# Attention and a SwiGLU block on one core: scores computed transposed, exponentials without the row maximum, and feed-forward blocks of 384 and 512 tokens

## The chip, the cores and the metric

The kernel runs on one core of a Trainium2 chip. The metric is the device time of one execution in microseconds (us), taken as the median of several runs. The core has a matrix engine (PE, whose weight loads are listed apart as PEld), a vector engine (DVE), a scalar engine (ACT), a general engine (POOL) and a queue engine (SP) that here only issues transfers. Each engine works through its own instructions in order and waits on the others through semaphores.

## What is computed

```python
# q, k, v: 8 batches x 12 heads x 448 tokens x 64;  g_q, g_k: 64
q_n, k_n = rmsnorm(q, g_q), rmsnorm(k, g_k)
scores = q_n @ k_n^T / 8
scores = scores - max(scores, axis=-1)
attn = exp(scores);  attn = attn / (sum(attn) + 1e-9)
x = (attn @ v), heads side by side: 3584 tokens x 768
g = x @ w_gate                     # 768 x 1536
h = g * sigmoid(g) * (x @ w_val)   # 768 x 1536
out = h @ w_out                    # 1536 x 768
```

All of it is in float32. The three weight matrices come in as float64 and are rounded to float32 on the chip.

## The kernel before

A batch's 448 tokens lie on 112 partitions, four to each. Heads are taken in pairs, so that two heads of 64 fill 128 partitions of the transposed queries and keys. A step of the attention is half the queries (two chunks of 112) of a pair of heads; a batch has 12 steps, the whole kernel 96.

In a step `softmax` computes four tiles of scores (L208, queries on the partitions), takes the maximum of each row on DVE (L218), lets ACT form the exponentials with that maximum as bias and sum them (L222), and DVE divides them (L224 to L229). One step later `transpose_p` transposes the 16 blocks of the exponentials on PE (L240) and copies them out of PSUM on DVE and ACT (L242), and `weighted_sum` multiplies them with the values (L252, the two heads on the two halves of the partitions) and copies the result to `xT` (L259). Before every second step `normalise` scales the next pair of queries and keys (squares on POOL L166, sums on DVE L168, the power -1/2 on POOL L171, products on POOL L175) and `transpose_qk` transposes them (L190, copies L194 and L196).

The feed-forward block takes the tokens of one batch at a time. `gate_value` computes a tile of 128 hidden units for 448 tokens: six matmuls with `wg` and six with `wv` (L268), the silu on ACT (L273) and the product on DVE (L274). `out_rows` computes 112 tokens by 384 outputs from 12 matmuls (L283), copies them (L291) and stores them from SP (L294).

The order of the work is the order in which the program calls these functions: nothing reorders it. In step i the calls are `softmax(i)`, `normalise`, one unit of the feed-forward block of the batch before, `transpose_p(i - 1)`, the other units, `weighted_sum(i - 1)`, `transpose_qk`. The first batch's attention has no feed-forward work beside it. Instead it carries the weights: 36 parts of 768 KB are loaded by SP into four buffers, and three times a step `weights_step` issues the rounding of a part (DVE L126, L134, L147, L148; ACT L137, L138; POOL L151, L152). The feed-forward block of the last batch runs alone at the end.

Of the kernel before, what the change touches and what calls it, by code (L numbers as in the profile page):

```python
# [9 lines left out]
F32 = mybir.dt.float32  # L10
U32 = mybir.dt.uint32
I64 = mybir.dt.int64
AF = mybir.ActivationFunctionType
ALU = mybir.AluOpType
AX = mybir.AxisListType


@with_exitstack
def kernel(
    ctx: ExitStack,  # L20
    tc: tile.TileContext,
    q: bass.AP,
# [31 lines left out]
    NF = DFF // P  # L54
    HALF = DM // 2
    STEPS = 2 * NPAIR
    # The high word of 2**-126 as a float64, the least normal float32, read as a float32.
    TINY = 2.0**-15 * 1.125

    const = ctx.enter_context(tc.tile_pool(name="const", bufs=1))  # L60
# [33 lines left out]
        nc.sync.dma_start(vt[m].rearrange("p h j d -> p h (j d)"), pair_rows(v, m))  # L94

    def weight_parts():
        """Parts of the weights as they come in, and where they go."""
        gate, val = (w.rearrange("(c p) f -> p c f", p=P) for w in (moe_w_gate, moe_w_val))
        for c in range(NW):
            for half in range(2):  # L100
                for w, dst in ((gate, wg), (val, wv)):
                    yield w[:, c, ts(half, DFF // 2)], dst[:, c, ts(half, DFF // 2)]
        rows = moe_w_out.rearrange("(f p) c -> p f c", p=P)
        for f in range(NF):
            yield rows[:, f, :], wo[:, f, :]
# [5 lines left out]
            nc.sync.dma_start(raw, src)  # L111
            staged.append((raw.bitcast(U32).rearrange("p (n two) -> p n two", two=2), dst))

    # round_high and round_low make of a part's float64 bits the nearest float32. The float32 of
    # the high word's 20 bits of the fraction takes the high word's sign and first bit of the
    # exponent, and the bits behind the exponent's next three, which are all the first one's
    # opposite wherever the value is a normal float32; smaller values become 0. The low word times
    # its unit is added to that, and the sum is rounded.

    def round_high():  # L120
        if not staged:
# [35 lines left out]
        load_weights()  # L157

    def normalise(m):
        """Scales the pair's queries and keys by 1 / sqrt(sum of squares + 64 eps), that is by  # L160
        their inverse rms over 8; gg makes up for both eighths."""
        t = prep.tile([R, NJ, 2, 2, D], F32, name="qkn")
        sq = t.rearrange("p j x h d -> p (j x h d)").rearrange("p (g d) -> p g d", d=D)
        src = qk.pop(m)
        flat = src.rearrange("p x h j d -> p (x h j) d")
        nc.gpsimd.tensor_tensor(out=sq, in0=flat, in1=flat, op=ALU.mult)  # L166
        ss = prep.tile([R, 2 * 2 * NJ], F32, name="ss")
        nc.vector.tensor_reduce(out=ss, in_=sq, axis=AX.X, op=ALU.add)  # L168
        nc.vector.tensor_scalar_add(ss, ss, D * 1e-6)  # L169
        rr = prep.tile([R, 2, 2, NJ, 1], F32, name="rr")  # L170
        nc.gpsimd.tensor_tensor(  # L171
            out=rr.rearrange("p x h j one -> p (x h j one)"), in0=ss, in1=minus_half, op=ALU.pow
        )
        for x in range(2):
            nc.gpsimd.tensor_tensor(  # L175
                out=t[:, :, x].rearrange("p j h d -> p h j d"),
                in0=src[:, x],
                in1=rr[:, x].to_broadcast([R, 2, NJ, D]),
                op=ALU.mult,
            )  # L180
        qkn[m] = t
# [112 lines left out]
            nc.sync.dma_start(tokens[j], outsb.pop((b, j)))  # L294

    def ffn_plan(b):
        """The block's units by step: two hidden tiles a step in the first half, then the output's."""
        units = [[lambda f=f: gate_value(b, f) for f in (2 * n, 2 * n + 1)] for n in range(NF // 2)]
        outs = [lambda j=j, h=h: out_rows(b, j, h) for j in range(NJ) for h in range(2)]
        rest = STEPS - len(units)  # L300
        for n in range(rest):
            units.append(outs[n * len(outs) // rest : (n + 1) * len(outs) // rest])
        return units
# [54 lines left out]
            fn()  # L358


# [1 line left out]
_INS = ["q", "k", "v", "g_q", "g_k", "moe_w_gate", "moe_w_val", "moe_w_out"]  # L362
_OUTS = [((3584, 768), "float32")]
# [25 lines left out]
```

## Time and profile before

| | |
|---|---|
| median of 3 runs | 2389.96 us (2389.5 to 2390.48) |
| profiled execution, first to last instruction | 2387.6 us |
| PE busy | 2096.2 us, 88% |
| DVE busy | 945.6 us, 40% |
| ACT busy | 595.8 us, 25% |
| POOL busy | 479.3 us, 20% |
| first feed-forward matmul starts at | 342.4 us |
| transfers | 73.69 MB, 31 GB/s on average |

The profile lists groups of instructions by line and engine with their number, busy time and mean duration. It draws the span in 40 slices, with the share of the time an engine is busy in tenths and a row for the clock that PE was granted (9 is 90% and more of full speed). One float32 matmul of the program appears as two records on PE, a transpose as one. A timeline merges neighbouring records: the first number is the start, the second the length.

### The profile page before, as it was taken

What the parts mean: (1) busy time and instruction counts of PE and PEld (TensorE: products, weight loads), DVE (VectorE), ACT (ScalarE), POOL (GpSimd) and SP (SyncE); (2) the same over time, 40 slices, a digit from 0 to 9 for tenths busy, and PEclk for the clock granted to TensorE, in tenths of its full rate; (3) what the DMA queues carried; (4) which work ended last, traced back from release to release, by engine and by line L of the source; (5) the groups of instructions that cost most, each with busy time, mean ns of one, the idle gap of its engine ahead of it and who ended that gap; (6) DMA issues with size and microseconds to landing.
All of it is one profiled execution on the core that took longest, in us unless ns stands there. A gap on an engine that the chain in (4) does not pass through costs nothing.

```text
span 2387.6 us, 20461 instructions
## 1 busy us (share of the span) xinstructions
PE 2096.2 (88%) x8064; PEld 1111.7 (47%) x8064; DVE 945.6 (40%) x1713; ACT 595.8 (25%) x1246; POOL 479.3 (20%) x271
## 2 busy tenths in 40 slices
PE   3445469999999999999999999999999999999999
PEld 1222234455545554455445554455444554455555
DVE  6778853344233433344233433344233433332000
ACT  2333332322222222322222222322222222321000
POOL 5656641121111111121111111121111111110000
PEclk9655569999999999999999999999999999999999
DMA  3333300010000010000000010010000010000000
GB/s 123 107 102 93 126 27 12 12 29 24 18 23 12 24 35 12 12 30 24 18 24 12 24 35 12 12 30 24 18 24 12 24 35 12 12 22 12 6 0 24
DMA packets 44257, 73.69 MB, mean 31 GB/s; under 512 B 3712, under 2 KB 35968, under 8 KB 44160
## 3 DMA queue, kind: packets, MB, share of 16 engines
q1 hardware_dynamic: 43840, 72.37, 10.1%
q8 instruction: 64, 1.05, 0.2%
q14 instruction: 33, 0.27, 0.0%
q10 hardware_dynamic: 320, 0.00, 0.0%
HBM read 61.34 MB, written 11.01 MB: 30 GB/s over the span
## 4 chain that ended last, share of the span: by engine, by line
PE 76%; DVE 6%; ACT 3%; issue 1%; POOL 0%; DVEq 0%; ACTq 0%
PE mm L268 37%; PE mm L283 21%; PE sc L208 7%; PE av L252 6%; PE tr L240 4%; ACT p L222 3%; DVE nmax L218 2%; DVE pt L242 2%; PE tr L190 2%; DVE gt L274 1%; ACT pt L242 1%; DVE outsb L291 1%; POOL raw L151 0%; DVE wo L147 0%; DVE p L229 0%
## 5 line engine op out<-in xcount | busy, mean ns | idle before, releaser
L283 PE MATMUL mm<-wo,gt 128*112 128x384 f32 x1536 | 508.5, 488 | 0.0
L268 PE MATMUL mm<-xT,wg 128*128 128x448 f32 x1152 | 453.8, 543 | 0.0
L268 PE MATMUL mm<-xT,wv 128*128 128x448 f32 x1152 | 448.6, 539 | 0.0
L208 PE MATMUL sc<-KT,QT 64*112 64x448 f32 x768 | 282.8, 603 | 139.7 <-ACT p L222 138.9
L283 PEld LDWEIGHTS mm<-wo,gt 128*112 128x112 f32 x1536 | 267.2, 177 | 234.9 <-issue 28.0
L222 ACT ACTIVATE p<-sc,nmax 112x448 f32<-112x448 f32 x384 | 239.6, 630 | 495.7 <-DVE nmax L218 495.7
L171 POOL TENSOR_TENSOR rr<-ss,minus_half 112x16 f32<-112x16 f32 x48 | 142.7, 2972 | 1020.1 <-DVE ss L169 1020.1
L274 DVE TENSOR_TENSOR gt<-gt,mm 128x448 f32<-128x448 f32 x96 | 59.6, 621 | 676.0 <-PE mm L268 676.0
L268 PEld LDWEIGHTS mm<-xT,wv 128*128 128x128 f32 x1152 | 218.9, 190 | 214.1 <-issue 212.6
L240 PE MATMUL tr<-ident,p 112*112 112x112 f32 x1536 | 205.3, 279 | 121.0 <-DVE pt L242 113.1
L268 PEld LDWEIGHTS mm<-xT,wg 128*128 128x128 f32 x1152 | 212.1, 190 | 210.7 <-issue 210.5
L218 DVE TENSOR_REDUCE nmax<-sc 112x1 f32<-112x448 f32 x384 | 221.7, 618 | 127.3 <-PE sc L208 123.2
L240 PEld LDWEIGHTS tr<-ident,p 112*112 112x112 f32 x1536 | 166.6, 142 | 195.7 <-DVE pt L242 135.7
L242 ACT COPY pt<-tr 112x448 f32<-112x448 f32 x192 | 102.0, 531 | 508.4 <-PE tr L240 508.4
L208 PEld LDWEIGHTS sc<-KT,QT 64*112 64x112 f32 x768 | 90.3, 181 | 278.1 <-ACT p L222 210.8
L252 PE MATMUL av<-pt,v 112*64 112x224 f32 x1536 | 208.6, 387 | 4.3 <-ACT pt L242 4.3
L166 POOL TENSOR_TENSOR qkn<-qk 112x1024 f32<-112x1024 f32 x48 | 90.8, 1892 | 547.5 <-DMA qk<-in_k_dram 530.7
L242 DVE COPY pt<-tr 112x448 f32<-112x448 f32 x192 | 119.0, 620 | 125.8 <-PE tr L240 125.8
L252 PEld LDWEIGHTS av<-pt,v 112*64 112x64 f32 x1536 | 117.7, 147 | 96.3 <-issue 38.7
L229 DVE TENSOR_SCALAR p<-p,rsum 112x448 f32<-112x448 f32 x384 | 147.9, 449 | 3.4
L273 ACT ACTIVATE gt<-mm 128x448 f32<-128x448 f32 x96 | 52.1, 543 | 346.2 <-PE mm L268 346.2
L259 DVE COPY xT<-av 128x224 f32<-128x224 f32 x96 | 37.5, 391 | 239.1 <-PE av L252 239.1
(40 smaller groups left out, 988.2 us busy)
## 6 DMA issues: line engine op xcount, KB each, us to landing
qk<-in_q_dram SPq DMA_DIRECT2D x48, 224.0 KB, 3.7
qk<-in_k_dram SPq DMA_DIRECT2D x48, 224.0 KB, 3.7
v<-in_v_dram SPq DMA_DIRECT2D x48, 224.0 KB, 2.9
out_dram<-outsb SPq DMA_DIRECT2D x32, 336.0 KB, 2.7
raw<-in_moe_w_gate_dram SPq DMA_DIRECT2D x12, 768.0 KB, 4.6
raw<-in_moe_w_val_dram SPq DMA_DIRECT2D x12, 768.0 KB, 4.4
raw<-in_moe_w_out_dram SPq DMA_DIRECT2D x12, 768.0 KB, 4.4
gq<-in_g_q_dram ACTq DMA_DIRECT2D x2, 0.2 KB, 3.5
```

What stands on the lines that cost most here:

```text
L166: nc.gpsimd.tensor_tensor(out=sq, in0=flat, in1=flat, op=ALU.mult)
L171: nc.gpsimd.tensor_tensor(out=rr.rearrange("p x h j one -> p (x h j one)"), in0=ss, in1=minus_half, op=ALU.pow)
L208: nc.tensor.matmul(sc, QT[m][rows, 2 * half + jl, :], KT[m][rows].rearrange("p j r -> p (j r)"), start=True, stop=True,)
L218: nc.vector.tensor_reduce(out=nmax[:, at], in_=scs[hh], axis=AX.X, op=ALU.max, negate=True)
L222: nc.scalar.activation(p, scs[hh], AF.Exp, bias=nmax[:, at], accum_out=den[:, at])
L229: nc.vector.tensor_scalar(out=p, in0=p, scalar1=rsum[i][:, ds(2 * jl + hh, 1)], scalar2=None, op0=ALU.mult)
L240: nc.tensor.transpose(ps[0:R, j, :], p[:, ts(j, R)], ident[0:R, 0:R])
L242: copy(PT[i, hh][:, :, jl, :], ps[0:R])
L252: nc.tensor.matmul(av[ds(64 * hh, 64), :], vt[m][:, hh, j, :], PT[i, hh][:, j].rearrange("p a r -> p (a r)"), start=(j == 0), stop=(j == N ...
L268: nc.tensor.matmul(t, w[:, c, ts(f, P)], xT[b][:, c, :], start=(c == 0), stop=(c == NW - 1))
L274: nc.vector.tensor_tensor(out=g, in0=g, in1=ps[1], op=ALU.mult)
L283: nc.tensor.matmul(ps[0:R, 0:HALF], gt[b][:, f, ts(j, R)], wo[:, f, ts(half, HALF)], start=(f == 0), stop=(f == NF - 1),)
```

## The change

The old kernel stays in the program under the name `general`. A new function `fast` runs first. A guard takes the largest product of the two gains, and after `fast` all engines read a flag: if that product is above 8, `general` runs as well; otherwise its instructions are branched over. In the reference's inputs the largest product is 5.26.

`fast` computes the same result in another way:

- The scores are transposed: keys lie on the partitions, queries along the free dimension. The exponentials (one ACT instruction for two heads, 896 elements) are then already in the layout in which the weighted sum takes them, so the 1536 transposes of the exponentials and their copies are gone.
- No row maximum is subtracted. The maxima on DVE and the division of the exponentials are gone. The four tiles of exponentials of a pair are added up on POOL (three additions of 896 elements), a matmul with ones sums them over the partitions, and DVE takes the reciprocal and multiplies the weighted sum by it.
- A pair of heads is two slots. The even slot transposes the next pair's queries and keys, computes half the scores and the weighted sum of the pair before; the odd slot computes the other half and divides.
- The squares move from POOL to ACT, and the copy of the transposed keys from DVE to ACT.
- The feed-forward block takes two batches (896 tokens) as a block of 384 and one of 512 tokens. Output tiles have 128 tokens in place of 112: 56 tiles of 12 matmuls in place of 64. The silu is computed from a tanh on ACT, with one more DVE operation.
- The attention of the next two batches is spread over the first half of the 384 block (12 slots, one after every second unit) and the second half of the 512 block (12 slots over 16 half units). The other two halves and the last 512 block run with no attention beside them.
- The weights come in by groups of 256 hidden units, through the buffer `gt` in place of buffers of their own. A part is rounded by two instructions on ACT and four on DVE (none on POOL); the addition is an integer one on 16-bit halves. 20 of the 36 parts are rounded within the 14 slots that come before the first feed-forward unit, the rest between the first units.
- Outputs are stored from ACT's queue in place of SP's.

On PE in the steady part, before: the names are `mm` for the feed-forward tiles, `tr` for transposes, `av` for the weighted sum, `sc` for scores. The rows around the end of a step, from the first half of a feed-forward block:

```order
L268 MATMUL mm<-xT,wv 128x448 x6
L240 MATMUL tr<-ident,p 112x112 x16
L268 MATMUL mm<-xT,wg 128x448 x6
L268 MATMUL mm<-xT,wv 128x448 x6
L252 MATMUL av<-pt,v 64x224 x8
L190 MATMUL tr<-ident,qkn 128x112 x8
L208 MATMUL sc<-KT,QT 112x448 x4
L268 MATMUL mm<-xT,wg 128x448 x6
L268 MATMUL mm<-xT,wv 128x448 x6
L240 MATMUL tr<-ident,p 112x112 x16
```

The same place after the change, from the first half of a 384 block (L622 is the feed-forward matmul, L539 the transposes of queries and keys, L555 the scores, L575 the weighted sum, L588 the sum by ones):

```order
L555 MATMUL st<-QT,KT 112x448 x4
L588 MATMUL at<-sums,ones 64x448 x2
L622 MATMUL mm<-xT,wg 128x384 x6
L622 MATMUL mm<-xT,wv 128x384 x6
L539 MATMUL at<-ident,t 128x112 x8
L555 MATMUL st<-QT,KT 112x448 x4
L575 MATMUL at<-e,v 64x448 x8
L622 MATMUL mm<-xT,wg 128x384 x6
L622 MATMUL mm<-xT,wv 128x384 x6
```

The 32 transposes of the exponentials of a pair are gone, the two weighted sums of 224 columns have become one of 448, a sum by ones is new, and a slot stands after two feed-forward units instead of being split by them.

On DVE while the first batch's weights are rounded, before: L147 to L134 is the rounding of one part, L218 to L229 the softmax of a step.

```order
L147 SCALAR_TENSOR_TENSOR wg<-raw,wg 128x768
L148 TENSOR_SCALAR raw<-wg 128x768
L126 TENSOR_SCALAR wv<-raw 128x768
L134 SCALAR_TENSOR_TENSOR wv<-raw,wv 128x768
L218 TENSOR_REDUCE nmax<-sc 112x1 x4
L224 TENSOR_SCALAR den<-den 112x4
L225 RECIPROCAL rsum<-den 112x4
L229 TENSOR_SCALAR p<-p,rsum 112x448 x4
L168 TENSOR_REDUCE ss<-qkn 112x16
L169 TENSOR_SCALAR ss<-ss 112x16
```

After, in the slots before the first feed-forward unit (L482 to L494 is one part, L590 and L591 the division of a pair, L544 to L516 the next pairs' queries and sums of squares):

```order
L590 RECIPROCAL inv<-at 128x448
L591 TENSOR_TENSOR xT<-at,inv 128x448
L482 TENSOR_SCALAR wv<-wv 128x768
L483 TENSOR_SCALAR wv<-wv 128x768
L491 SCALAR_TENSOR_TENSOR wv<-gt,wv 128x768
L494 ISA wv<-gt,wv 128x1536
L544 TENSOR_SCALAR QT<-at,gg 128x448
L515 TENSOR_REDUCE ss<-t 112x16
L516 TENSOR_SCALAR ss<-ss 112x16
```

A pair of heads leaves five DVE instructions where it left 30, the addition of a weight part comes from POOL to DVE (L494), and the reciprocal of a whole tile is new.

The diff, cut to what the steps below speak of:

```diff
+def fast(ctx, tc, q, k, v, g_q, g_k, moe_w_gate, moe_w_val, moe_w_out, out):
+    BLOCKS = ((0, 384), (384, 512))
+    ps_st = ctx.enter_context(tc.tile_pool(name="ps_st", bufs=2, space=bass.MemoryType.PSUM))
+    ps_at = ctx.enter_context(tc.tile_pool(name="ps_at", bufs=2, space=bass.MemoryType.PSUM))
+    ps_mm = ctx.enter_context(tc.tile_pool(name="ps_mm", bufs=2, space=bass.MemoryType.PSUM))
...
+    def load_weights():
+        if not parts:
+            return
+        n = parts[0][0]
+        slot = n % 4 if n < 20 else 2 + n % 2
+        if any(slot == other[0] for other in staged):
+            return
...
+    def round_weights():
...
+        nc.scalar.activation(w, hi.bitcast(F32), AF.Abs)
+        nc.scalar.activation(lo, lo, AF.Copy, scale=2.0**-29)
+        nc.vector.tensor_scalar_max(w, w, LEAST)
+        nc.vector.tensor_scalar(out=bits, in0=bits, scalar1=3, scalar2=0x3FFFFFFF, ...)
+        nc.vector.scalar_tensor_tensor(bits, hi, 0xC0000000, bits, ...)
+        nc.vector.tensor_tensor(out=bits, in0=bits, in1=lo, op=ALU.add)
...
+    def scores(m, j):
+        st = ps_st.tile([P, 2, TB], F32, name="st")
+        for h in range(2):
+            rows = ds(D * h, D)
+            nc.tensor.matmul(st[0:R, h, 0:S], KT[m][rows, j, :], QT[m][rows]..., ...)
+        E[m, j] = attn.tile([R, 2, S], F32, name="e", bufs=5)
+        nc.scalar.activation(E[m, j], st[0:R, :, 0:S], AF.Exp)
+        if j == 1:
+            nc.gpsimd.tensor_tensor(out=sums[m], in0=E[m, 0], in1=E[m, 1], op=ALU.add)
+        elif j > 1:
+            nc.gpsimd.tensor_tensor(out=sums[m], in0=sums[m], in1=E[m, j], op=ALU.add)
...
+    def divide(m):
+        den = ps_at.tile([P, TB], F32, name="at")
+        for h in range(2):
+            nc.tensor.matmul(den[ds(D * h, D), 0:S], ones[0:R, :], s[:, h], ...)
+        nc.vector.reciprocal(inv, den[:, 0:S])
+        nc.vector.tensor_tensor(out=xT[...], in0=av.pop(m)[:, 0:S], in1=inv, op=ALU.mult)
+
+    def slot(i):
+        m, second = divmod(i, 2)
+        if not second:
+            transpose_qk(m + 1)
+        if m < NM:
+            for j in (0, 1):
+                scores(m, 2 * second + j)
+        if m > 0:
+            if second:
+                divide(m - 1)
+            else:
+                weighted(m - 1)
+                load_v(m + 1)
+        if not second:
+            normalise(m + 2)
+            load_qk(m + 3)
...
+    attend(PER + 2)                      # 14 slots; PER = 12
+    for n in range(B):
+        if n % 2 == 0:
+            mix(ups(n), PER)             # 24 units of 384 tokens, 12 slots between them
...
+            mix(downs(n), 0)
+        else:
+            mix(ups(n), 0)               # 24 units of 512 tokens
+            mix(downs(n), PER if n < B - 1 else 0)
...
+    fast(tc, *args)
+    fits = nc.values_load(fits[0:1, 0:1], min_val=0, max_val=1)
+    with tc.If(fits == 0):
+        general(tc, *args)
```

More of the change, by code (lines that the diff above doesn't have):

```diff
@@ L18, with general @@
 @with_exitstack
-def kernel(
+def general(
     ctx: ExitStack,
@@ new lines, with kernel @@
+@with_exitstack
+def kernel(
+    ctx: ExitStack,
+    tc: tile.TileContext,
+    q: bass.AP,
+    k: bass.AP,
+    v: bass.AP,
+    g_q: bass.AP,
+    g_k: bass.AP,
+    moe_w_gate: bass.AP,
+    moe_w_val: bass.AP,
+    moe_w_out: bass.AP,
+    out: bass.AP,
+):
+    nc = tc.nc
+    args = (q, k, v, g_q, g_k, moe_w_gate, moe_w_val, moe_w_out, out)
+    D = q.shape[3]
+    guard = ctx.enter_context(tc.tile_pool(name="guard", bufs=1))
+    g2 = guard.tile([1, 2, D], F32, name="g2")
+    gp = guard.tile([1, D], F32, name="gp")
+    top = guard.tile([1, 1], F32, name="top")
+    fits = guard.tile([1, 1], mybir.dt.int32, name="fits")
+    for i, x in enumerate((g_q, g_k)):
+        nc.scalar.dma_start(g2[:, i], x.rearrange("(one d) -> one d", one=1))
+    nc.vector.tensor_tensor(out=gp, in0=g2[:, 0], in1=g2[:, 1], op=ALU.mult)
+    nc.vector.tensor_reduce(
+        out=top, in_=gp, axis=AX.X, op=ALU.max, apply_absolute_value=True
+    )
+    nc.vector.tensor_scalar(out=fits, in0=top, scalar1=8.0, scalar2=None, op0=ALU.is_le)
+    fast(tc, *args)
+    fits = nc.values_load(fits[0:1, 0:1], min_val=0, max_val=1)
+    with tc.If(fits == 0):
+        general(tc, *args)
```

271 lines of the change are left out of this document (added).

## Prediction

> **What bounds the kernel now.** The page comes first: PE is the busiest engine, and the slices show two regimes.
>
> ```profile
> PE 2096.2 (88%) x8064; PEld 1111.7 (47%) x8064; DVE 945.6 (40%) x1713; ACT 595.8 (25%) x1246; POOL 479.3 (20%) x271
> PE   3445469999999999999999999999999999999999
> DVE  6778853344233433344233433344233433332000
> PEclk9655569999999999999999999999999999999999
> ```
>
> For the first six slices (60 us each) PE is at a third to a half and DVE at up to 80%; from then on PE is full. The stretches in numbers (columns: window, length, busy us and count of PE, PEld, DVE, ACT, POOL, then the granted clock, the DMA share, GB/s):
>
> ```profile
> 60.00:120.00 60.00, 25.33 (x92) 12.79 (x90) 46.45 (x61) 21.15 (x41) 38.58 (x20) 0.63 0.36 108
> 240.00:300.00 60.00, 26.17 (x93) 13.74 (x91) 47.73 (x64) 21.88 (x41) 37.99 (x19) 0.58 0.38 122
> 300.00:360.00 60.00, 41.38 (x147) 21.76 (x146) 33.89 (x54) 18.12 (x36) 24.31 (x13) 0.71 0.07 24
> 600.00:900.00 300.00, 283.82 (x1122) 150.57 (x1122) 107.91 (x212) 76.64 (x163) 42.89 (x25) 1.00 0.08 22
> ```
>
> Early on, DVE works 47 of 60 us on weights and softmax while PE waits at a clock of about 0.6. Later PE works 284 of 300 us at full clock. The chain of waits gives the borders, each row a start, a length and what ran:
>
> ```profile
> 342.40 9.23 PE mm L268 x24
> 610.87 9.23 PE mm L268 x24
> ```
>
> The first feed-forward matmul starts at 342.4 us, and a batch takes 610.87 − 342.40 = 268.5 us. PE's timeline shows what fills a step:
>
> ```profile
> 899.83 1.74 PE L252 MATMUL av<-pt,v 112*64 112x224 f32 x16
> 901.49 1.75 PE L208 MATMUL sc<-KT,QT 64*112 64x448 f32 x6
> 903.96 1.00 PE L208 MATMUL sc<-KT,QT 64*112 64x448 f32 x2 [0.72 <-ACT p L222]
> 904.90 4.78 PE L268 MATMUL mm<-xT,wg 128*128 128x448 f32 x12
> ...
> 914.02 0.93 PE L240 MATMUL tr<-ident,p 112*112 112x112 f32 x8
> 915.50 0.98 PE L240 MATMUL tr<-ident,p 112*112 112x112 f32 x8 [0.55 <-DVE pt L242]
> ...
> 927.11 0.99 PE L190 MATMUL tr<-ident,qkn 112*128 112x112 f32 x8
> 928.02 1.75 PE L208 MATMUL sc<-KT,QT 64*112 64x448 f32 x6
> ```
>
> A step waits twice, 0.72 and 0.55 us, 1.27 us together. The last block, with nothing beside it, gives the clean rates and the end:
>
> ```profile
> 2303.29 4.67 PE L268 MATMUL mm<-xT,wg 128*128 128x448 f32 x12
> 2307.80 4.67 PE L268 MATMUL mm<-xT,wv 128*128 128x448 f32 x12
> 2321.33 62.08 PE L283 MATMUL mm<-wo,gt 128*112 128x384 f32 x192
> 2383.49 0.48 ACT L291 COPY outsb<-mm 112x384 f32<-112x384 f32 x1 [15.00 <-PE mm L283]
> ```
>
> Six matmuls of 448 columns take 2307.80 − 2303.29 = 4.51 us, so a record of 448 columns 0.376 us. 192 records of 384 columns take 62.08 us, so 24 (an output tile) 7.76 us: again in proportion to the columns. The feed-forward work of a batch is thus 24 × 4.51 + 8 × 7.76 = 170.3 us, and the other 98.2 us of the 268.5 are attention: 16.4 us for each of six pairs of heads. After PE's end (2383.4) the span runs on for 4.2 us.
>
> **The change: feed-forward on PE.** Time goes by columns, so a unit of 384 tokens takes 4.51 × 384/448 = 3.87 us, one of 512 5.15 us. The 384 block: 24 × 3.87 + 6 × 7.76 = 139.4 us; the 512 block: 24 × 5.15 + 8 × 7.76 = 185.7 us; four of each: **1300 us**, against 8 × 170.3 = 1362. The saving is that of eight output tiles fewer.
>
> **Attention on PE.** The row of 16 records of 224 columns starts at 899.83 and the next at 901.49: 1.66 us. At the feed-forward rate 16 × 0.188 = 3.0 us would be needed one behind the other, so the two heads, which write different halves of the partitions, run side by side. So do the scores of two heads: six records in 1.75 us, end included, where one behind the other needs 2.26. For a pair of heads after the change I take: transposes 0.91 us (927.11 to 928.02); two slots of four score matmuls, each 2 × 0.75 plus 0.1 = 1.6, together 3.2; the weighted sum 4 × 0.75 plus the 0.17 that the row above has over its ideal, 3.2; the sum by ones 0.85. That is 8.2 us in place of 16.4. 42 of the 48 pairs' worth of slots (84 slots) lie beside feed-forward work: **343 us**.
>
> **What hides the rest there.** Exponentials and copies from PSUM go by these groups (busy, mean ns; for POOL and DVE the min/median/max):
>
> ```profile
> L222 ACT ACTIVATE p<-sc,nmax 112x448 f32<-112x448 f32 x384 | 239.6, 630 | 495.7 <-DVE nmax L218 495.7
> L273 ACT ACTIVATE gt<-mm 128x448 f32<-128x448 f32 x96 | 52.1, 543 | 346.2 <-PE mm L268 346.2
> L168 DVE TENSOR_REDUCE ss<-qkn 112x16 f32<-112x1024 f32 x48 | 58.2, 1212 | 0.0
> L196 DVE TENSOR_SCALAR KT<-tr,gg 128x448 f32<-128x448 f32 x48 | 32.3, 674 | 0.4 <-PE tr L190 0.4
> L166 POOL TENSOR_TENSOR qkn<-qk x48: 1887/1892/1898, 4.6 to 2110.0; 112x1024 f32<-112x1024 f32 x48
> L171 POOL TENSOR_TENSOR rr<-ss,minus_half x48: 2898/2899/3551, 8.8 to 2130.4; 112x16 f32<-112x16 f32 x48
> L175 POOL TENSOR_TENSOR qkn<-qk,rr x96: 1041/1042/1357, 11.7 to 2134.4; 112x512 f32<-112x512 f32 x96
> ```
>
> A pair now costs POOL three additions of 896 elements (1892 × 896/1024 = 1.66 us each), 2.9 for the power and 2 × 1.04: 10.0 us. ACT has four exponentials (543 ns for 448 columns; twice that is 1.09 us, 0.92 with the fixed part once), two squares (0.6), a copy: 5.5 us. The shortest time for a pair on PE is in the outputs of the 512 block, 8.2 + 2 × 4/3 × 3.88 = 18.5 us, so neither bounds. Between two slots lies at least one unit of 3.9 us, in which exponentials and the division finish. The waits of 0.72 and 0.55 lose their causes (a third score buffer awaited from ACT; transposes awaiting a copy). Late next would be the two `at` buffers, which wait for DVE's division. I charge **15 us** for that in all, between 0 and the old 1.27 us per slot. The stores on ACT's queue and SP's loads stand behind waits that end a slot or more before anyone needs them: nothing.
>
> **Before the first feed-forward unit.** 14 slots with 20 weight parts. DVE's prices:
>
> ```profile
> L126 DVE TENSOR_SCALAR wg<-raw x12: 551/553/554, 25.4 to 209.9; 128x768 uint32<-128x768 uint32 x12
> L134 DVE SCALAR_TENSOR_TENSOR wg<-raw,wg x12: 957/2101/2104, 26.0 to 210.5; 128x768 uint32<-128x768 uint32 x12
> L147 DVE SCALAR_TENSOR_TENSOR wg<-raw,wg x12: 949/1393/1489, 27.9 to 213.8; 128x768 f32<-128x768 f32 x12
> L224 DVE TENSOR_SCALAR den<-den x96: 169/171/1515, 22.2 to 2182.6; 112x4 f32<-112x4 f32 x96
> L225 DVE RECIPROCAL rsum<-den x96: 177/178/179, 22.4 to 2182.8; 112x4 f32<-112x4 f32 x96
> ```
>
> Per part: two one-source operations, 0.55 each; L491 like L134, 0.96 to 2.10, 1.6 taken; L494 is not in the trace: 1536 elements with two sources lie between twice L147's minimum less one fixed 0.17 (1.7 us) and twice L134's slow case (4.2); 2.2 taken, nearer to the fast case, since POOL has no weight work any more. Sum 4.9 us (3.8 to 7.0), 20 parts 98 us. A pair adds the reduction and its constant 1.4, the copy 0.67, a reciprocal and a product of 448 from PSUM at 0.7 each: 3.5 us, seven pairs 24 us. In the reciprocal, four elements cost 7 ns more than in a multiplication, some 1.8 ns each, so 448 lie between 0.67 and 1.2 us.
>
> The page "VectorE: DVE Perf Modes" of the Trainium skill, in its section "First, the fixed hardware budget", has the reciprocal run its divide steps with a repeat count of 8; the 178 ns beside 171 do not look like that, but rival 2 gives the case a time.
>
> The start is a chain (a timeline row of POOL's first products, and sizes with the time from issue to landing):
>
> ```profile
> 11.74 2.04 POOL L175 TENSOR_TENSOR qkn<-qk,rr 112x512 f32<-112x512 f32 x2
> ```
> ```profile
> qk<-in_k_dram SPq DMA_DIRECT2D x48, 224.0 KB, 3.7
> raw<-in_moe_w_gate_dram SPq DMA_DIRECT2D x12, 768.0 KB, 4.6
> ```
>
> The second pair's keys wait on SP for a buffer that the first product frees at 12.8 us, and the weights queue behind them. Keys landed 16.5, squares 17.7, sums 19.1, power 22.0, products 24.1, transposes and scores to 28: the first part is rounded at **28 us**. For the first four pairs, with two parts each, the ring from transposes and scores (0.91 and 1.6 at a clock of 0.6: 4.2 us) over an exponential (0.9), squares (1.2), the reduction behind other DVE work (4) and POOL's addition and power (4.6) to the products (2.1) takes 17 us, 18 with hand-overs, more than DVE's 13. For the last three, with four parts each, DVE's 4 × 4.9 + 3.5 = 23 us rule. 28 + 4 × 18 + 3 × 23 = 169: **170 us**. Low: 28 + 76 + 24 = 128. High: 28 + 140 + 24 = 192, with 4 of slack 196.
>
> **Behind it** the other 16 parts are rounded during the first 11 units: DVE has 16 × 4.9 + 3 × 3.5 + 11 × 0.7 = 97 us there, or 110 if SP, waiting for buffers of queries, holds back weights; PE has 11 × 3.87 + 2.75 × 8.2 = 65. I add **35 us** (5 to 70).
>
> **The end**: the old 4.2 us and a read flag with a branch over the old program, which no row shows: between 0 and 10, nearest to the barrier that ends the span now, 4. Together **8 us**.
>
> **Sum**: 170 + 35 + 1300 + 343 + 15 + 8 = 1871 us of span. The profiled span of 2387.6 is 2.4 under the median of 2389.96, so **1873 us**.
>
> **Rivals.**
>
> 1. DVE holds the opening longer: additions and products in their slow cases, +26 before the first unit and +35 behind it: 1934 us. For it: L134's median is its slow case. Against: POOL loses its weight work, beside which the slow cases lie. Chance 0.12.
> 2. The reciprocal is slow on a whole tile. At eight times the time per element of L196 it takes (0.67 − 0.17) × 8 + 0.17 = 4.2 us in place of 0.7: six in the opening, 21 us, and where only a unit of 3.88 us lies before the next use of its buffer the division's 4.9 us outlast it by 1.0, in some 12 of the 18 pairs beside outputs: +33, 1906 us. The Trainium skill's page named above has such a count. Against: L225's row. 0.10.
> 3. New waits in the slots as long as the old: 84 × 1.27 − 15 = +92: 1965 us. For it: two `at` buffers serve four uses a pair. Against: a unit lies between the slots. 0.08.
> 4. The change does not do what it says: the heads don't run side by side at 448 columns. A pair then costs 0.9 + 6.0 + 6.0 + 1.5 = 14.4, +6.2 × 42: 2133 us. Against: the same shapes of scores do so now. 0.04.
> 5. Slower than before: PE waits in each slot, is busy under some 70% and gets the clock of the early windows (0.71 at 41 of 60 us, 0.58 at 26). Mixed stretches hold 4 × 24 × 3.87 + 24 × 7.76 + 343 = 901 us at full clock; at 0.58 these take 1553: 2525 us. It turns to slower at a mean clock of 901/(901 + 517) = 0.64. Against: in the window from 600 us PE waits 5% and has 1.00. The Trainium skill's page "TensorE: Matmul & The Clock Gate", in the section "HAM oscillation — how this bites in real kernels", states that idle gaps beyond about 3.4 us bring back half the clock; the trace agrees as far as gaps of 0.7 us leave it at 1.00. 0.03.
> 6. `general` runs too: 1873 + 2388 = 4261 us. The inputs' largest product, 5.26, excludes it unless the guard errs. 0.01.
> 7. The opening at its low ends (−42, −30) and no waits (−15): 1786 us. 0.06 for less than 1800.
>
> **How the numbers follow.** My forecast, 1800 to 1950 us, has 0.56 of its own. With rivals 1 to 3 the range is 1800 to 1970, which leaves out 0.14. A measurement of this kernel can tell about 0.2% (5 us). Rivals 5 and 6 make slower 0.04; nothing lies within 0.2%; faster 0.96.
>
> **What would show it.** Right: the first feed-forward matmul near 170 us; 384 units 3.87 us apart; a pair of slots some 8 us on PE; L494 near 2.2 us; clock 1.00 from about 280 us on; no wait of PE with a total over 20 us after that. Wrong: L590 near 3.8 us; PE waiting on DVE or POOL in the slots; score records one behind the other; lines of `general` in the trace.

## The result, and the profile after

The changed kernel takes 1930.3 us (median of 4 runs, 1928.94 to 1932.59) against 2389.75 us: a ratio of 0.8078, 95% interval 0.8066 to 0.8089. The forecast was 1873 us with a range of 1800 to 1970. The page of the changed kernel:

```profile
span 1929.4 us, 14302 instructions
PE 1773.2 (92%) x5760; PEld 867.0 (45%) x5760; DVE 530.3 (27%) x580; ACT 382.1 (20%) x561; POOL 550.6 (29%) x296
PE   4557669999989999999999899999999899999998
PEclk9778779999999999999999999999999899999999
```

A slice is now 48 us. PE is full from the seventh slice on, but not quite as evenly as before: here and there an 8 stands among the nines. The chain of waits gives the borders (start, length, what ran):

```profile
354.93 46.64 PE mm L648 x144
401.56 123.60 PE mm L622 x288
...
803.37 46.64 PE mm L648 x144
...
1862.19 61.93 PE mm L648 x192
```

A half block of outputs that runs alone takes 46.64 us, the 512 units that run alone 123.60, the last outputs 61.93. Between 525.16 (401.56 + 123.60) and 803.37 lies a stretch with attention in it, 278.2 us; there are two more, from 973.6 to 1250.2 and from 1420.4 to 1692.0. PE's timeline has the first feed-forward matmul:

```profile
147.55 3.49 PE L622 MATMUL mm<-xT,wg 128*128 128x384 f32 x10
```

So the span shrank by 458.2 us: 342.40 − 147.55 = 194.9 in the opening and 264.5 behind it (PE's end at 2383.4 and at 1924.1, less those starts), and 1.1 came back at the end. Against the forecast's terms, with the version of the second experiment below in the last column:

| part of the span, us | forecast | after | two tiles for the sums |
|---|---|---|---|
| up to the first feed-forward matmul | 170 | 147.6 | 136.6 |
| first 24 tiles of the 384 units (142 of PE's work + 35) | 177 | 207.4 | 180.2 |
| the parts without attention | 743 | 742.9 | 742.9 |
| three stretches with attention (3 × 253.4 + 15) | 775 | 826.3 | 770.4 |
| end | 8 | 5.3 | 5.3 |
| sum | 1873 (the prediction rounds its terms to 1871) | 1929.4 | 1835.4 |

The 57 us that the forecast lacked are thus +30 in the first units and +51 in the three stretches, less 22 in the opening and 3 at the end. A look into the first of the stretches, on PE and POOL (start, length, engine, line; in brackets the wait before it and what ended it):

```profile
545.11 4.14 PE L648 MATMUL mm<-wo,gt 128*128 128x384 f32 x12
545.37 2.08 POOL L566 TENSOR_TENSOR sums<-e 112x896 f32<-112x896 f32 x1 [179.01 <-ACT e L563]
547.40 2.91 POOL L518 TENSOR_TENSOR rr<-ss,minus_half 112x16 f32<-112x16 f32 x1
550.39 2.04 POOL L522 TENSOR_TENSOR t<-qk,rr 112x512 f32<-112x512 f32 x2
551.49 0.60 PE L539 MATMUL at<-ident,t 112*128 112x112 f32 x4 [2.24 <-POOL t L522]
552.49 1.01 PE L539 MATMUL at<-ident,t 112*128 112x112 f32 x4 [0.40 <-POOL t L522]
553.43 3.33 PE L555 MATMUL st<-QT,KT 64*112 64x448 f32 x8
556.69 4.27 PE L575 MATMUL at<-e,v 112*64 112x448 f32 x16
...
571.67 2.08 POOL L566 TENSOR_TENSOR sums<-e 112x896 f32<-112x896 f32 x1 [15.04 <-PE at L588]
```

The sums of a pair live in a pool with one buffer. The first addition of a pair (L566) overwrites the tile that the sum by ones of the pair before (L588, which ended at 545.1) reads, so it cannot start earlier, although its exponentials are there: the last of them ended at 537.3, so ACT, which the first row names, did not end that wait. For the next pair, at 571.67, the row names L588. Behind L566, in POOL's order, stand the power and the products of the next queries and keys: 2.03 + 2.99 + 1.05 us later the first half of the products is ready, 6.3 us after L588. In the output part there is one unit of 4.14 us in between, so PE waits 2.24 us, then 0.40 for the other half. Then the scores take 3.33 us, where elsewhere they take 1.76, and the weighted sum 4.27 where elsewhere it takes 3.23. The stretches in numbers show the clock that PE was granted there (third number from the right): 0.91 over 60 us, where the forecast expected 1.00, and 0.66 over the 10 us with these slow rows.

```profile
552.00:562.00 10.00, 9.60 (x33) 3.78 (x33) 2.04 (x3) 3.40 (x5) 4.55 (x3) 0.66 0.09 24
540.00:600.00 60.00, 54.73 (x193) 25.67 (x192) 14.90 (x12) 13.41 (x19) 29.42 (x17) 0.91 0.14 40
```

The view of waits has POOL's wait (us in total, times, longest):

```profile
POOL sums L566 <- PE at L588: 244.4, 21, 28.2
```

### The profile page after: what moved, and what is told of

The parts are those of the page before. It is cut to its first block, busy times and chain, and to the rows that moved or that the text cites. A ratio compares the mean times of both kernels' runs of the same rounds, so it can differ in the third digit from the quotient of the medians.

```text
span 1929.4 us, 14302 instructions
## 1 busy us (share of the span) xinstructions
PE 1773.2 (92%) x5760; PEld 867.0 (45%) x5760; DVE 530.3 (27%) x580; ACT 382.1 (20%) x561; POOL 550.6 (29%) x296
## 4 chain that ended last, share of the span: by engine, by line
PE 85%; POOL 5%; DVE 5%; issue 3%; ACT 1%; DMA 1%; POOLq 0%; SPq 0%; DVEq 0%; ACTq 0%
PE mm L622 44%; PE mm L648 20%; PE st L555 9%; PE at L575 8%; POOL rr L518 3%; POOL t L522 2%; PE at L539 2%; PE at L588 2%; DVE inv L590 1%; DMA gt<-in_moe_w_out_dram 1%; ACT e L563 1%; DVE wg L494 0%; DVE wg L483 0%; DVE wo L494 0%; DVE wg L491 0%
## 5 line engine op out<-in xcount | busy, mean ns | idle before, releaser
L622 PE MATMUL mm<-xT,wg 128*128 128x512 f32 (+1 forms) x1152 | 455.4, 544 | 7.8 <-DVE xT L591 7.8
L622 PE MATMUL mm<-xT,wv 128*128 128x512 f32 (+1 forms) x1152 | 450.4, 541 | 0.0
L648 PE MATMUL mm<-wo,gt 128*128 128x384 f32 x1344 | 444.0, 489 | 0.0
L566 POOL TENSOR_TENSOR sums<-e 112x896 f32<-112x896 f32 x48 | 102.2, 2129 | 1094.8 <-ACT e L563 850.5
L648 PEld LDWEIGHTS mm<-wo,gt 128*128 128x128 f32 x1344 | 252.3, 190 | 195.2 <-issue 27.3
L622 PEld LDWEIGHTS mm<-xT,wg 128*128 128x128 f32 x1152 | 214.8, 190 | 244.6 <-issue 168.3
L622 PEld LDWEIGHTS mm<-xT,wv 128*128 128x128 f32 x1152 | 219.9, 191 | 215.3 <-issue 139.9
L563 ACT ACTIVATE e<-st 112x896 f32<-112x896 f32 x192 | 170.9, 916 | 215.1 <-PE st L555 167.2
L568 POOL TENSOR_TENSOR sums<-sums,e 112x896 f32<-112x896 f32 x96 | 206.7, 2153 | 16.8 <-ACT e L563 12.9
L555 PE MATMUL st<-QT,KT 64*112 64x448 f32 x768 | 195.5, 633 | 0.1
L590 DVE RECIPROCAL inv<-at 128x448 f32<-128x448 f32 x48 | 141.9, 2956 | 162.8 <-PE at L588 162.8
L575 PE MATMUL at<-e,v 112*64 112x448 f32 x768 | 167.3, 581 | 16.5 <-ACT KT L548 16.5
L539 PE MATMUL at<-ident,t 112*128 112x112 f32 x384 | 61.5, 306 | 126.6 <-POOL t L522 80.1
L539 PEld LDWEIGHTS at<-ident,t 112*128 112x128 f32 x384 | 47.6, 163 | 153.3 <-POOL t L522 96.3
L575 PEld LDWEIGHTS at<-e,v 112*64 112x64 f32 x768 | 54.1, 146 | 132.5 <-issue 106.2
L555 PEld LDWEIGHTS st<-QT,KT 64*112 64x112 f32 x768 | 68.8, 195 | 83.8 <-issue 66.7
```

The lines of the kernel that those rows point to most:

```text
L539: nc.tensor.transpose(ps[:, ts(j, R)], t[:, j, x].rearrange("p h d -> p (h d)"), ident[0:R, 0:R])
L555: nc.tensor.matmul(st[0:R, h, 0:S], KT[m][rows, j, :], QT[m][rows].rearrange("p j r -> p (j r)"), start=True, stop=True,)
L563: nc.scalar.activation(E[m, j], st[0:R, :, 0:S], AF.Exp)
L566: nc.gpsimd.tensor_tensor(out=sums[m], in0=E[m, 0], in1=E[m, 1], op=ALU.add)
L568: nc.gpsimd.tensor_tensor(out=sums[m], in0=sums[m], in1=E[m, j], op=ALU.add)
L575: nc.tensor.matmul(av[m][ds(D * h, D), 0:S], vt[m][:, h, j, :], e[:, h], start=(j == 0), stop=(j == NJ - 1),)
```

## Experiments

The theory after this reading, S: the one tile of the sums costs about 65 us, most of it in the three stretches. Rivals: P, POOL simply has too much work; D, the reciprocal costs the time (2.96 us in place of the 0.7 charged); and that the 57 us lie in other parts, the guard, the tanh or the loads.

**The control.** Two tiles for the sums need space, so two other tiles go: tanh is written into `gt`, the reciprocal into `xT`.

```diff
-        inv = attn.tile([P, S], F32, name="inv")
-        nc.vector.reciprocal(inv, den[:, 0:S])
...
+        to = xT[:, c, ds(b % 2 * S, S)]
+        nc.vector.reciprocal(to, den[:, 0:S])
+        nc.vector.tensor_tensor(out=to, in0=av.pop(m)[:, 0:S], in1=to, op=ALU.mult)
...
-            t = ffn.tile([P, TB], F32, name="tanh", bufs=1)
-            nc.scalar.activation(t[:, 0:size], ps[:, 0:size], AF.Tanh, scale=0.5)
+            nc.scalar.activation(g, ps[:, 0:size], AF.Tanh, scale=0.5)
```

> A control: the tanh is written into the tile of hidden units and the reciprocal into the tile of attention results, which frees two small buffers and moves no instruction. All theories: 1930 us as for the changed kernel, within 3 us.

1928.37 us (1927.75 to 1929.54), ratio 0.8071 (0.8057 to 0.8084). The edit by itself does nothing that can be measured.

**Two tiles for the sums**, on top of the control:

```diff
-            sums[m] = attn.tile([R, 2, S], F32, name="sums")
+            sums[m] = attn.tile([R, 2, S], F32, name="sums", bufs=2)
```

> The same with two tiles for the sums of the exponentials in place of one. Theory S (single tile): POOL's first addition of a pair waits for the sum by ones of the pair before, and the power and the products behind it in POOL's queue come too late for PE's next transposes. Then PE's waits for POOL beside the outputs go (278, 277 and 272 us from the start of the outputs of a 512 block to the end of the next 384 block's hidden units become 256 to 259), the opening loses some 10 of its 178 us, and the time is 1865 us (1855 to 1880). Rival P (POOL simply has too much work, 11.4 us a pair): PE still waits for POOL, 1915 to 1930 us. Rival D (the slow division holds the two PSUM buffers): no change, 1930 us.

1837.85 us (1837.3 to 1839.65), ratio 0.7693 (0.768 to 0.7706): 90.5 us less than the control, and the fastest version here that leaves nothing out. Its chain of waits has the border of the first outputs 38.1 us earlier, and the first stretch, 363.44 + 123.60 to 745.47, takes 258.4 us in place of 278.2:

```profile
316.80 46.64 PE mm L645 x144
363.44 123.60 PE mm L620 x288
745.47 46.64 PE mm L645 x144
```

The three stretches together lose 826.3 − 770.4 = 55.9 us; with the 38.1 that is the whole difference of the spans, 94.0. On PE and POOL, the place that was shown above:

```profile
499.24 2.09 POOL L566 TENSOR_TENSOR sums<-e 112x896 f32<-112x896 f32 x1 [178.76 <-ACT e L563]
...
504.80 2.04 POOL L522 TENSOR_TENSOR t<-qk,rr 112x512 f32<-112x512 f32 x2
506.99 4.14 PE L645 MATMUL mm<-wo,gt 128*128 128x384 f32 x12
510.96 0.93 PE L539 MATMUL at<-ident,t 112*128 112x112 f32 x8
511.82 1.76 PE L555 MATMUL st<-QT,KT 64*112 64x448 f32 x8
```

The products end at 506.84, before the unit that precedes the transposes starts; no wait is left there, the scores have their 1.76 us, and the granted clock from 505 to 516 us is 1.00. Theory S is shown, and rival P falls: POOL has the same work. The gain lies outside the expected range, because the opening and the first units gained 38.1 us where 10 were put down for them.

**No reciprocal** (a copy in its place, so these two kernels leave out the division by the sum), with one tile for the sums and with two:

```diff
-        nc.vector.reciprocal(inv, den[:, 0:S])
+        nc.vector.tensor_copy(out=inv, in_=den[:, 0:S])
```

> The changed kernel with a copy in place of the reciprocal (0.6 us in place of 2.96; the division by the sum is left out). Theory S: the reciprocal matters only while DVE is full, in the opening and the first units after it: 8 to 10 of them at 2.3 us, 1907 to 1920 us, and the stretches beside the outputs keep their 272 to 278 us. Rival D: these stretches lose 5 us a pair, 1930 - 20 - 60 = 1850 us. Rival P: as theory S.

1928.42 us (1927.59 to 1934.43), ratio 0.8076 (0.8061 to 0.809): nothing, where 10 to 23 us were expected. The groups of instructions show that the operation did become short, first in the changed kernel, then without the reciprocal (min/median/max in ns):

```profile
L590 DVE RECIPROCAL inv<-at 128x448 f32<-128x448 f32 x48 | 141.9, 2956 | 162.8 <-PE at L588 162.8
```
```profile
L590 DVE COPY inv<-at x48: 610/625/626, 50.4 to 1689.6; 128x448 f32<-128x448 f32 x48
```

DVE lost 48 × 2.33 = 112 us of work, and the kernel none. In the three stretches PE's waits are for POOL's products with or without the reciprocal (826.3 and 825.3 us in all). Before them, PE's waits for the division got shorter and those for the products longer: over the whole run 46.2 became 29.5 us, and 80.1 became 90.3. Rival D falls; why the last periods of the opening, which wait for DVE, got no shorter was not taken apart.

> Two tiles for the sums and a copy in place of the reciprocal (the division by the sum is left out). Theory S: the two gains add, as they lie in different places except for the opening: 1840 to 1865 us. Rival P: 1900 to 1920 us. Rival D: as without the reciprocal alone, 1850 us.

1827.73 us (1826.3 to 1828.14), ratio 0.7648 (0.7636 to 0.7661): 10.1 us less than with the reciprocal, 9.8 of it ahead of the first outputs (these start at 307.0 in place of 316.8 us). The reciprocal has a price once the sums have two tiles, and nearly all of it while weights are rounded on the same engine (the three stretches give 1.7 us).

**The reciprocal on ACT**, with two tiles, as a logarithm and an exponential:

```diff
-        nc.vector.reciprocal(to, den[:, 0:S])
+        nc.scalar.activation(to, den[:, 0:S], AF.Ln)
+        nc.scalar.activation(to, to, AF.Exp, scale=-1.0)
```

> Two tiles for the sums as in e1_sums2 (1837.9 us), and the reciprocal on ACT: the logarithm of the sum (from PSUM), then the exponential of its negative. DVE loses 2.96 us a pair, ACT gains two operations of 448 columns, about 1.1 us, and where the logarithm lies in another table than the exponential two table loads of 1.28 us (the length that the loads have in the run with the Silu function). Theory F (DVE's work before the first output tile is what the reciprocal costs, as the run without it showed): 1828 (1825 to 1832). Rival T (the loads and the two operations stand in front of the exponentials of the next slot, and PE waits for these): 3.7 us in each of 24 slots that have only one unit behind them would be up to +20, 1838 to 1858.

1841.36 us (1840.44 to 1843.2), ratio 0.7708 (0.7695 to 0.7721). Gain and cost were both there. The first outputs start at 308.9 us, 7.9 earlier, as theory F had it; but each stretch takes 3.7 us more (487.04 to 745.47 has become 479.16 to 741.28, 258.4 and 262.1). On ACT and on PE in the first stretch:

```profile
520.33 1.28 ACT L590 ACT_TABLE_LOAD   x1
521.63 0.54 ACT L590 ACTIVATE xT<-at 128x448 f32<-128x448 f32 x1
522.19 1.28 ACT L591 ACT_TABLE_LOAD   x1
523.49 0.58 ACT L591 ACTIVATE xT<-xT 128x448 f32<-128x448 f32 x1
```
```profile
524.87 0.58 PE L539 MATMUL at<-ident,t 112*128 112x112 f32 x4 [0.62 <-DVE xT L592]
599.92 0.91 PE L621 MATMUL mm<-xT,wg 128*128 128x384 f32 x2 [1.55 <-DVE xT L592]
```

The division comes 3.7 us after the two exponentials that stand ahead of it, and PE waits for one of its two `at` buffers, which the forecast had named as what would be late next. Not the exponentials behind the loads, as rival T had it, but the division itself is late.

**Parts that cost nothing.** The guard with its branch and the old program (left out), and the silu by tanh (the Silu function and a plain product in its place):

> The changed kernel without the flag, the branch and the old kernel behind it. The prediction charged 4 us for them (0 to 10). The trace now has 5.3 us between PE's end and the end of the span, against 4.2 before the change, so 1 us or less is expected: 1929 us (1926 to 1931). Rival: a long program costs instruction loading all through the run, 1915 us or less.

> One part of the change undone: the silu by ACT's own function and one product on DVE, in place of tanh and two operations. Some 96 table loads of 1.28 us come back on ACT, all beside the 384 blocks' hidden units. Theory: ACT has a fifth of its time in use and a slot has two units of 3.9 us to finish, so nothing is seen there; in the first units, where ACT also rounds weights, 0 to 10 us: 1930 to 1940 us. Rival: the loads delay the exponentials on PE's path, 2.6 us a slot in 48 slots, 2050 us.

1928.15 us (ratio 0.8069, 0.8055 to 0.8082) and 1927.51 us (1915.28 to 1929.08, ratio 0.8048, 0.8021 to 0.8075): neither differs measurably from the changed kernel. The second has 99 table loads of 1.28 us more than the changed kernel's one, 50 on the silu's line and 49 on the exponential's (L563). These 127 us of loads cost nothing that can be measured on an engine that is busy 20% of the span in the changed kernel; the tanh saves them and gains nothing by it.

**Without the row maximum alone**, in the old kernel:

```diff
-                nc.vector.tensor_reduce(
-                    out=nmax[:, at], in_=scs[hh], axis=AX.X, op=ALU.max, negate=True
-                )
...
-                nc.scalar.activation(p, scs[hh], AF.Exp, bias=nmax[:, at], accum_out=den[:, at])
+                nc.scalar.activation(p, scs[hh], AF.Exp, accum_out=den[:, at])
```

> One part of the change alone, in the kernel before: no row maximum (the reduction on DVE is gone, the exponentials take no bias), all else as it was. Theory: PE's 0.72 us wait of a step goes with it (84 steps, 60 us), the opening of 342 us gets up to 30 us shorter as DVE loses 2.5 us of a step; the transposes of the exponentials stay. 2300 us (2280 to 2330): the smaller part of the 460 us. Rival: the maximum was what held all, and the transposes cost little: below 2150 us.

2315.56 us (2315.04 to 2316.34), ratio 0.9689 (0.9672 to 0.9705): 74 of the 459 us. The first feed-forward matmul starts at 330.8 in place of 342.4 us, and a batch takes 259.4 in place of 268.5. On PE's timeline the wait of 0.72 us is gone from the scores, twelve times a batch, and that of 0.55 has stayed:

```profile
871.80 2.73 PE L207 MATMUL sc<-KT,QT 64*112 64x448 f32 x8
...
885.07 0.98 PE L236 MATMUL tr<-ident,p 112*112 112x112 f32 x8 [0.55 <-DVE pt L238]
```

The other 385 us come with the rest of the change: the transposed layout, the order of the work and the larger blocks, which no run takes apart.

**Four buffers for queries and keys**, with two tiles for the sums (the room comes from the output rows, one buffer instead of two):

```diff
-                qk[m, x] = io.tile([R, 2, NJ, D], F32, name="qk", bufs=3)
+                qk[m, x] = io.tile([R, 2, NJ, D], F32, name="qk", bufs=4)
```

> Two tiles for the sums, and four buffers for queries and keys in place of three (room for it from one buffer for the output rows). Theory Q: in the opening and the first units SP holds the loads of weights behind the load of the next keys, whose buffer comes free only after POOL's products; ACT then waits for weights with the copy of the keys behind it, and PE for that copy. With the fourth buffer these waits go: the first units (180 us with two sums tiles, PE's own work 143) lose 15 to 25 us, the opening 5 to 10, 1838 - 20 to 35 = 1803 to 1818 us. Rival V (DVE's work alone sets the opening and the first units): 1835 us, within 4.

1840.98 us (1839.75 to 1843.35), ratio 0.7706 (0.7693 to 0.7719). SP's wait for that buffer up to 320 us fell from 78.7 to 15.9 us, but PE's waits there stayed (89 and 91 us in all), and the time is 3 us longer. Theory Q falls: with two tiles for the sums, taking this wait off SP gains nothing. Rival V's 1835 us, within 4, is missed by 2.

**How much of the price is waiting, and how much the clock.** Idle powers on POOL in front of the products put the wait back into the version with two tiles, in a dose, from pair 18 on: three of them (16, 16 and 8 columns), two of them (16 and 16), or 16, 16 and 4.

```diff
+        if m >= 3 * NPAIR:
+            idle = prep.tile([R, 2 * 2 * NJ], F32, name="idle", bufs=1)
+            nc.gpsimd.tensor_tensor(
+                out=idle[:, 0:16], in0=ss[:, 0:16], in1=minus_half[:, 0:16], op=ALU.pow
+            )
...
```

> Two tiles for the sums, and from the pair 18 on POOL does 7.4 us of idle work (three powers into a spare tile) ahead of the products of each pair, so that they come as late as in the changed kernel. Theory C: PE then waits 2.2 us before transposes that follow after one unit, and the scores behind run at half clock (8 records in 3.3 us in place of 1.76), as in the changed kernel: 9 to 10 such places at 5.2 us, 1838 + 47 = 1885 us (1870 to 1895). Rival: the low clock had another cause, then the places cost the wait alone, 2.6 us each: 1863 us.

> The same with two powers, 5.9 us, so that PE's wait is about 0.8 us at the same places. Theory C: such a wait is too short to lower the clock (the kernel before waited 0.72 us and kept it), the scores stay at 1.76 us, 10 places at 1.2 us: 1850 us (1840 to 1855). Rival: any wait ahead of transposes lowers the clock: 1870 us.

> e8_late_2 with the third idle power over 4 columns instead of 8: by the lengths of 16 columns (2.90 us) and 8 (1.64) it takes 1.0 us, so the products come 0.65 us earlier than in e8_late_2 and PE's first wait at the five places is about 1.6 us (there 2.2, in e9_late_1 0.5), with 0.4 between the two halves as in both. Theory C1 (a first wait of 1.6 us already halves the clock): scores of 3.3 us at these places as in e8_late_2, and 5 x 0.65 less time than it, 1858 (1855 to 1861). Theory C2 (it doesn't yet): scores of 1.76 us, and e9_late_1 plus 5 x 1.1, 1851 (1848 to 1853).

1861.39 us (1859.03 to 1863.76, 2 runs; ratio 0.7791, 0.7768 to 0.7815), 1845.23 us (1844.6 to 1845.86, 2 runs; 0.7723, 0.7701 to 0.7746) and 1855.83 us (1854.88 to 1856.71; 0.7767, 0.7754 to 0.778). One place of each on PE (the transposes with the first wait, and the scores behind them): with three powers, with two, and two places with the small third one:

```profile
571.63 0.60 PE L550 MATMUL at<-ident,t 112*128 112x112 f32 x4 [2.22 <-POOL t L533]
...
573.34 3.23 PE L566 MATMUL st<-QT,KT 64*112 64x448 f32 x8
```
```profile
943.04 0.60 PE L547 MATMUL at<-ident,t 112*128 112x112 f32 x4 [0.50 <-POOL t L530]
...
944.57 1.76 PE L563 MATMUL st<-QT,KT 64*112 64x448 f32 x8
```
```profile
947.12 0.60 PE L550 MATMUL at<-ident,t 112*128 112x112 f32 x4 [1.59 <-POOL t L533]
...
948.66 3.10 PE L566 MATMUL st<-QT,KT 64*112 64x448 f32 x8
...
1007.97 0.60 PE L550 MATMUL at<-ident,t 112*128 112x112 f32 x4 [1.59 <-POOL t L533]
...
1009.50 1.76 PE L566 MATMUL st<-QT,KT 64*112 64x448 f32 x8
```

Behind each first wait shown stands a second one of 0.40 us, for the other half. Each kernel has such waits at five places in the three stretches, the changed kernel at twelve. From the start of the first wait to the scores PE ran eight transposes there and no ordinary matmul. Sorted by that length (from the timelines):

| from the last ordinary matmul to the scores | places | scores slower than 1.76 us | cost of a place against the version with two tiles |
|---|---|---|---|
| 2.0 us (two powers) | 5 | 0 | 1.3 us |
| 3.1 us (small third power) | 5 | 2 | 2.4 us where the scores kept 1.76 us, 4.1 where they were slow |
| 3.8 to 4.3 us (three powers) | 5 | 5 | 4.7 to 5.2 us |
| 3.8 to 4.2 us (the changed kernel) | 12 | 10 | 4.7 us |

Theory C, that the wait costs more than its length because the clock falls behind it, is shown by these rows, not by the total: the 1861 us are also what the rival had (1863), but with 10 places at 2.6 us, where the trace has five at 4.9. The expectation of 1885 us counted twice the places. Of the 55.9 us, the waits that PE's timeline lists at the twelve places are 30.3 (2.24 and mostly 0.40 at each), and the other 25.6, by difference, are slow matmuls behind them. Between C1 and C2 neither holds: at the same 3.1 us two places were slow and three not, and the time lies between their 1858 and 1851, inside C1's range. The Trainium skill's page "TensorE: Matmul & The Clock Gate" bears on this at two places: its section "What's actually happening" has the clock decided by windows of 3.4 us that run freely, and its section "Part 4: PE-mode transpose" says that transposes don't count as work for it in the same way. The runs agree as far as gaps with nothing but transposes of 3.8 us and more lost the clock 15 times in 17, of 2.0 us never, and of 3.1 us sometimes, below the page's figure. Whether a freely running window decides which of equal gaps loses the clock, and whether the transposes in them count as work, was not tried.

## Why the prediction was right, and where it was short

**The rates held.** A unit of 512, a half block of outputs and the last outputs were forecast at 123.6, 46.6 and 62.1 us and took 123.60, 46.64 and 61.93. A pair of heads costs 0.86 + 1.69 + 3.16 + 1.69 + 0.90 = 8.3 us on PE (transposes, scores, weighted sum, scores, sum by ones, starts to starts), forecast 8.2; the two heads do run side by side. So the 1300 and the 343 us, and with them the sign and most of the size, were right, and rivals 4 and 6 are out. Worked out from these rates, an estimate: the attention beside feed-forward work takes some 42 × (16.4 − 8.3) = 340 us less on PE, the feed-forward work 62 less, the opening is 195 shorter, and new waits take some 130 back; that is 467, against 458 measured.

**"I charge 15 us for that in all": this step failed.** The waits in the slots cost 51 us more. It said that late next would be the two `at` buffers, and took POOL as not bounding because its 10.0 us for a pair fit into 18.5. That is a rate; the trace shows a delay. POOL may begin a pair's additions only when PE's sum by ones of the pair before is over, and the next pair's power and products stand behind them on POOL, so they end 6 to 7 us after it, wherever PE is by then. Rival 3, new waits in the slots, was right in kind, with a wrong buffer; it took a wait at its length alone and at every slot, where it was twelve places at 4.7 us. With two tiles for the sums, the stretches take 770.4 us, and the 15 us would have been enough. Rival 5's falling clock came about in the stretches only behind these waits, for 25.6 us.

**"I add 35 us" behind the opening: 65 in its place**, by the same buffer. There it reaches further, as the chain of waits shows (start, length, what ran):

```profile
188.81 0.07 POOL sums L566
...
190.84 2.92 POOL rr L518
...
194.90 0.31 SPq L436
...
195.31 4.25 DMA gt<-in_moe_w_out_dram
...
202.79 2.64 DVE wo L494
205.43 2.88 DVE inv L590
```

L566, held back for 28 us until L588, delays the products, these free the buffer for which SP's load of the next keys waits, the weights' loads stand behind that on SP, and DVE's division behind the rounding of those weights; PE's transposes then wait 11.9 us for the `at` buffer. With two tiles this term measures 180.2 − 142 = 38 us, so the 35 was the right size for the kernel that it described.

**The opening: 170 forecast, 147.6 measured.** The prices held better than the count. PE's transposes mark the pairs:

```profile
35.03 1.01 PE L539 MATMUL at<-ident,t 112*128 112x112 f32 x4 [6.09 <-POOL t L522]
...
53.63 1.01 PE L539 MATMUL at<-ident,t 112*128 112x112 f32 x4 [7.50 <-POOL t L522]
...
136.33 1.72 PE L539 MATMUL at<-ident,t 112*128 112x112 f32 x8 [12.30 <-DVE inv L590]
```

From 35.0 to 136.3 us there are five periods (18.6 at first, 23.3 at last), 101.3 us, where three of 18 and two of 23 are 100. But 28 + 4 × 18 + 3 × 23 counts seven whole ones: at 28 us the first pair was already half done (7 us to 35.0 in place of 18), and the last has no period behind it, only its own two slots (11.2 in place of 23). That is 23 us too many, less 1.3. The end of the range there is also too low: the slow cases of a part's four operations sum to 1.1 + 2.1 + 4.2 = 7.4 us, not 7.0. That the forecast came as close as 57 us is in part luck: with the opening counted right it would have been 1851, 79 us short. For the kernel with two tiles, which it in effect described, it was 36 us too high (1871 against 1835.4 of span), nearly all of it in the opening (170 against 136.6).

**Sizes that were off and cost little.** The addition L494 was taken at 2.2 us. Two rows of DVE, and what POOL did beside each of them:

```profile
127.85 0.96 DVE L494 CUSTOM_DVE_ANT_0 wg<-gt,wg 128x1536 uint16<-128x1536 uint16 x1
202.79 2.64 DVE L494 CUSTOM_DVE_ANT_0 wo<-gt,wo 128x1536 uint16<-128x1536 uint16 x1
```
```profile
126.26 3.22 POOL L518 TENSOR_TENSOR rr<-ss,minus_half 112x16 f32<-112x16 f32 x1
202.14 5.22 POOL L568 TENSOR_TENSOR sums<-sums,e 112x896 f32<-112x896 f32 x2 [6.27 <-ACT e L563]
```

It takes 0.96 us beside POOL's power, as it does alone (at 211.15), and 2.6 where it starts during one of POOL's additions, 11 times in 36; before the first unit its mean is 1.8. So rival 1 did not come. The reciprocal was taken at 0.7 us and takes 2.96: the row of four elements misled (and the 1.8 ns more an element that the prediction reads from it give 0.67 + 448 × 0.0018 = 1.5 us, not its 1.2), and the rule of the page "VectorE: DVE Perf Modes" of the Trainium skill, repeated steps, had the right direction and, at 4.2 us, rival 2's reading of it too much. It cost nothing that can be measured here, as the run without it shows. The end took 5.3 us in place of 8, and the guard in it nothing that can be measured.

## What to carry to other kernels

Ask of each buffer with one tile who frees it, and then what is queued behind the instruction that waits for it on its engine: an engine that is busy 29% still held PE here, because its next, unrelated work stood behind a wait. Compare such a chain's length from its release with the work that PE has in between, not the engine's busy time with PE's. A wait of PE can cost near twice its length if the clock falls behind it, so short waits in an otherwise full stretch are worth looking for first: one more tile of 3.5 KB a partition gave 90 us.

## What the runs showed of the hardware that was not expected

- Waits of 2.2 and 0.4 us around four transposes were mostly enough to slow the next matmuls (15 places in 17, scores 2.6 to 3.3 us in place of 1.76); waits of 0.5 and 0.4 were not (none in 5).
- A reciprocal of 448 float32 elements per partition from PSUM takes 2.96 us on DVE, a copy of the same 0.63: 6.6 ns an element against 1.4.
- An integer addition on DVE (1536 elements of 16 bits) takes 0.96 us alone or beside POOL's power, and 2.6 where it starts during a POOL addition of 896 elements.
- Table loads on ACT take 1.28 us each, and the next instruction starts within 0.02 us of their end.
